# A projection's 64-row rests, run as pairs on both halves of the array

## The chip, the cores and the metric

The kernel runs on one core of one Trainium2 chip. The metric is device time in microseconds (us) of one execution. Of the kernel before, three timed runs gave a median of 467.6 us (466.76 to 468.47).

Engines by the profile's names: PE is TensorE's matmul, PEld its weight load, DVE is VectorE, ACT is ScalarE, POOL is GpSimd, SP is SyncE, which issues nearly all the DMAs. PE works with 128 rows of the array, or with the rows split into halves (64) or quarters (32); a matmul on a part of the rows leaves the other parts free for another.

## The reference

Two blocks in sequence over x of 2048 tokens and width 576, both on a layer-normed input with a residual:

```python
h  = x + attention(layernorm(x))      # 32 heads of width 18
h2 = h + mlp(layernorm(h))            # 576 -> 4608, gelu, -> 576
# attention, per segment s of 512 tokens (4 in all):
#   logits = q k^T * 18**-0.5 + causal mask ; a_dot = softmax(logits) v
#   a_mem  = phi(q) M / (phi(q) z + 1e-6)     phi(t) = t + 1 if t > 0 else exp(t)
#   o = sigmoid(beta) * a_mem + (1 - sigmoid(beta)) * a_dot
#   then M += phi(k)^T v,  z += sum phi(k)
#   attention = concat(o) @ wo,  with q, k, v = x @ wq, x @ wk, x @ wv
```

All arrays are bfloat16. The width of 576 matters here: it is four blocks of 128 and a rest of 64, and every product over the width (q, k, v, wo, the MLP's first layer) has such a rest.

## The kernel before

**Tiling.** The tokens are cut into 8 chunks of 256 (two tiles of 128). Two chunks make one segment of the attention. A chunk passes through these streams, each a Python generator that issues operations:

- `stream_P(tl)`: layer norm of a token tile (DVE, with POOL for the power), its transpose `xT` (for the first two chunks through PE and a copy, from the third on by a transposing DMA, `dma_t`), and the q, k, v projection. The output is 1728 columns wide. The first chunk cuts it into 6 pieces of 288 columns, all later ones into 4 pieces of 432 (`CH`). A piece is five matmuls into one PSUM bank: `mm5` (line 549) issues four with 128 rows (line 551) and one for the rest (line 552). This last one has 65 rows (`KTAIL`) and not 64: row 64 of the weights is a row of zeros, and with 65 rows the matmul counts as one over the whole array. The piece is then copied out of the bank by ACT or DVE (`move`, lines 631 and 632), into `qk_pad` and `v_aug`; q and k are transposed into `QT` and `KT`.
- `stream_A`: the attention. `scores` (line 752) computes 16 small matmuls on 32 rows each, four side by side; ACT takes the exponential of all of them (line 758, 2048 columns); POOL or DVE masks; `weighted` (line 784) multiplies with v. `memory_mm` (line 807) and `stream_M` (line 710) are the memory's reads and updates.
- `stream_B(tl)`: the product with wo (also `mm5`), residual, second layer norm and its transpose.
- `stream_F1`, `stream_F2`: the MLP's two layers. F1 takes its rests first, in pairs on 64 rows: `tails` (line 1048) lets the upper and the lower half of the rows work at the same time, each into its own bank; then come four matmuls of 128 rows for each (line 1061). For this the upper rows, 64 to 127, hold a second copy of the rest of the input: the second layer norm (line 573) writes its last 64 columns twice. F1 of the first chunk is done by lines 1021 and 1023, F2 by line 1110.

**PSUM.** There are 8 banks: four for the scores (`st`), one for the attention's sums (`ox`) and three (`bank0` to `bank2`) that all other products share. After the last attention the four score banks join those three as `late`.

**The order.** A planner (`step`, lines 1135 to 1183) runs all streams against estimated durations and due times (`SLACK`, `PHASES`) and picks each engine's next operation. It also chooses the bank of each product (`bank_slots.take()`). Where PE would have nothing to do early on, it puts in fillers (line 1179), matmuls of 256 columns over a zeroed tile `pq`. Then `arranged` (line 1197) moves operations by a table (`MOVES`): pairs of numbers, the operation and the one after which it goes; an operation can also go to another engine this way. What results is one fixed order for each engine, and each engine works through its own in that order.

Of the kernel before, what the change touches and what calls it, by code (L numbers as in the profile page):

```python
# [9 lines left out]
ALU = mybir.AluOpType  # L10
# [6 lines left out]
def kernel(  # L17
# [41 lines left out]
    def sbuf(name, shape, dt=BF16):  # L59
# [77 lines left out]
    MOVES = dict(PE=[74, -1, 71, 73, 77, 71, 81, 78, 75, 81, 85, 75, 89, 80, 93, 89, 86, 82, 90, 84, 83, 88, 97, 83, 94, 97, 102,  # L137
# [30 lines left out]
                                      ACT=[59, 53, 61, 54, 45, 113, 124, 120, 135, 124, 55, 130, 155, 145, 168, 171, 224, 218, 56,  # L168
# [7 lines left out]
                                      DVE=[18, 14, 24, 40, 17, 24, 30, 31, 36, 32, 101, 36, 35, 33, 19, 35, 39, 41, 46, 39, 139,  # L176
# [71 lines left out]
    port_op = [None]  # L248
    fetched = []
    writer, readers, known = {}, {}, {}  # L250

    class Op:
        start, end, at, apart, two, hold, ways = None, NEVER, None, False, False, 0.0, None

# [1003 lines left out]
```

## Time and profile before

| | before |
|---|---|
| median of three runs | 467.6 us (466.76 to 468.47) |
| profiled execution | 467.02 us |
| its span, first to last instruction | 465.1 us |
| PE busy | 459.2 us (99%), 6102 matmuls |
| ACT busy | 320.0 us (69%) |
| DVE busy | 272.9 us (59%) |
| POOL busy | 180.0 us (39%) |
| mean share of the DMA engines, GB/s | q1: 69.7%; 174 GB/s |

A group line of the profile names the line of the kernel, the engine, the operation, what it writes and reads, the shapes, the count (x), and then the busy time, the mean duration of one in ns and the idle time ahead of it. PE's matmuls are pipelined: one lasts longer than the distance to the next, so that the busy time of a group is no sum of durations, and the distance of two starts in the timeline tells what a matmul costs the stream. Each timeline line merges neighbours of one kind and has start, time covered, engine, line, operation, what is written and read, shapes and count.

### The profile page before, as it was taken

What the parts mean: (1) busy time and instruction counts of PE and PEld (TensorE: products, weight loads), DVE (VectorE), ACT (ScalarE), POOL (GpSimd) and SP (SyncE); (2) the same over time, 40 slices, a digit from 0 to 9 for tenths busy, and PEclk for the clock granted to TensorE, in tenths of its full rate; (3) what the DMA queues carried; (4) which work ended last, traced back from release to release, by engine and by line L of the source; (5) the groups of instructions that cost most, each with busy time, mean ns of one, the idle gap of its engine ahead of it and who ended that gap; (6) DMA issues with size and microseconds to landing.
All of it is one profiled execution on the core that took longest, in us unless ns stands there. A gap on an engine that the chain in (4) does not pass through costs nothing.

```text
span 465.1 us, 14420 instructions
## 1 busy us (share of the span) xinstructions
PE 459.2 (99%) x6102; PEld 351.6 (76%) x6102; DVE 272.9 (59%) x712; ACT 320.0 (69%) x299; POOL 180.0 (39%) x240
## 2 busy tenths in 40 slices
PE   8999999999999999999999999999999999999997
PEld 6777787777677777767677777678778788888885
DVE  4889878787874355777755647687345524212020
ACT  3987788977888877966768778658778453423620
POOL 4567233778563144487442116474233401000000
PEclk9999999999999999999999999999999999999999
DMA  8889699887598557587876645989956595747211
GB/s 210 251 257 293 127 205 192 177 216 153 130 220 205 167 148 222 129 164 150 152 178 184 176 154 149 169 192 196 229 168 178 167 215 169 155 126 222 68 40 51
DMA packets 123152, 80.89 MB, mean 174 GB/s; under 512 B 57536, under 2 KB 121040, under 8 KB 123088
## 3 DMA queue, kind: packets, MB, share of 16 engines
q1 hardware_dynamic: 123056, 79.98, 69.7%
q8 instruction: 47, 0.77, 0.7%
q0 software_dynamic: 32, 0.01, 0.1%
q14 instruction: 17, 0.14, 0.1%
HBM read 60.03 MB, written 7.08 MB: 144 GB/s over the span
## 4 chain that ended last, share of the span: by engine, by line
PE 96%; DMA 2%; DVE 1%; SPq 0%; issue 0%
PE bank L1110 25%; PE bank L1061 22%; PE bank L551 14%; PE ox L784 7%; PE st L752 6%; PE late L1110 5%; PE late L1061 4%; PE bank L1048 4%; PE bank L552 3%; DMA wqkv<-in_A_wq_dram 2%; PE bank L1021 1%; PE ox L1110 1%; PE bank L807 1%; PE bank L670 1%; PE ox L1061 1%; PE bank L710 1%
## 5 line engine op out<-in xcount | busy, mean ns | idle before, releaser
L758 ACT ACTIVATE pt<-st 128x2048 bf16<-128x2048 f32 x80 | 150.2, 1878 | 56.8 <-PE st L752 51.5
L1110 PE MATMUL bank<-w_sb,hT 128*128 128x288 bf16 x936 | 135.9, 286 | 0.0
L1110 PEld LDWEIGHTS <-hT 128*128 128x128 bf16 x1152 | 109.1, 98 | 26.9 <-issue 1.1
L1071 DVE TENSOR_TENSOR hT<-bank,b1T 128x512 bf16<-128x512 f32 x78 | 53.8, 689 | 69.0 <-PE bank L1061 68.5
L1061 PE MATMUL bank<-xn2T,w1g 128*128 128x256 bf16 x688 | 87.9, 273 | 0.0
L1061 PEld LDWEIGHTS <-w1g 128*128 128x128 bf16 x768 | 70.6, 98 | 16.0 <-issue 6.7
L763 POOL TENSOR_SCALAR_AFFINE_SELECT pt<-pt 128x512 bf16<-128x512 bf16 x84 | 54.1, 657 | 71.2 <-ACT pt L758 66.3
L1083 ACT ACTIVATE hT<-hT 128x1536 bf16<-128x1536 bf16 (+3 forms) x24 | 66.0, 2764 | 16.4 <-DVE hT L1071 16.2
L551 PE MATMUL bank<-wqkv,xT 128*128 128x432 bf16 (+1 forms) x268 | 57.1, 336 | 0.7 <-DMA wqkv<-in_A_wq_dram 0.7
L551 PEld LDWEIGHTS <-xT 128*128 128x128 bf16 x400 | 36.5, 97 | 19.7 <-issue 0.9
L784 PEld LDWEIGHTS <-pt 128*128 128x128 bf16 x1280 | 42.2, 96 | 4.5 <-issue 0.6
L784 PE MATMUL ox<-v_aug,pt 128*128 128x19 bf16 x1280 | 44.1, 172 | 0.0
L752 PE MATMUL st<-QT,KT 32*128 32x128 bf16 x1280 | 32.4, 217 | 0.6 <-issue 0.6
L799 POOL TENSOR_TENSOR pq<-ek,pq 128x512 bf16<-128x512 bf16 x24 | 27.9, 1162 | 12.6 <-DVE ek L797 10.8
L752 PEld LDWEIGHTS <-KT 32*128 32x128 bf16 x1280 | 18.5, 92 | 16.2 <-issue 14.3
L829 POOL TENSOR_TENSOR o_nat<-t,t 128x288 bf16<-128x288 f32 x24 | 19.9, 830 | 25.7 <-DVE t L828 25.6
L1069 ACT ACTIVATE hT<-bank,b1T 128x256 bf16<-128x256 f32 x62 | 25.8, 473 | 5.6 <-PE bank L1061 4.6
L1061 PEld LDWEIGHTS <-wqkv 128*128 128x128 bf16 x272 | 26.0, 98 | 4.5 <-issue 0.4
L1110 PE MATMUL late<-w_sb,hT 128*128 128x288 bf16 x180 | 25.0, 286 | 0.0
L795 POOL TENSOR_SCALAR pq<-QT 128x512 bf16<-128x512 bf16 x24 | 15.4, 641 | 24.7 <-PE bank L807 9.9
L569 POOL TENSOR_TENSOR rstd_b<-rstd_b,mhalf 128x1 f32<-128x1 f32 x16 | 9.6, 602 | 39.2 <-DVE rstd_b L564 39.2
L931 POOL TENSOR_TENSOR h_t<-h_t,b_bc 128x576 f32<-128x576 f32 x16 | 20.7, 1296 | 6.0 <-DVE xn L573 4.8
(136 smaller groups left out, 620.1 us busy)
## 6 DMA issues: line engine op xcount, KB each, us to landing
w1g<-in_B_w_dram SPq DMA_DIRECT2D x50, 512.0 KB, 4.3
wqkv<-in_B_w_dram SPq DMA_DIRECT2D x17, 512.0 KB, 4.1
w_sb<-in_B_w_dram SPq DMA_DIRECT2D x6, 864.0 KB, 6.0
hd<-h_t SPq DMA_DIRECT2D x16, 288.0 KB, 3.0
hc<-hd SPq DMA_DIRECT2D x32, 144.0 KB, 2.8
w1g<-in_B_w_dram SPq DMA_DIRECT2D x100, 32.0 KB, 3.1
x_b<-in_A_x_dram SPq DMA_DIRECT2D x18, 144.0 KB, 3.7
hT<-in_B_w_dram SPq DMA_DIRECT2D x5, 512.0 KB, 5.6
```

What stands on the lines that cost most here:

```text
L551: nc.tensor.matmul(out=out_ap, lhsT=lhsT_of(slice(0, P), k), rhs=rhs_of(slice(0, P), k), start=(k == 0), stop=False)
L752: nc.tensor.matmul(out=st4[:, i, n * P:(n + 1) * P], lhsT=KTs[(c - c % 2 + kt // 2) % 3][rows, g, (kt % 2) * P:(kt % 2 + 1) * P], rhs=QTs[ ...
L758: op("ACT", 1.88, lambda: nc.scalar.activation(out=pt[:], in_=st4[:], func=ACT.Exp, scale=scale), sk, [("pt", slot, n) for n in range(4)], ...
L763: either(("POOL", 0.64, lambda part=part: nc.gpsimd.affine_select(out=part, in_=part, pattern=[[0, 4], [1, P]], compare_op=ALU.is_ge, fill ...
L784: nc.tensor.matmul(out=oxv[:, 4 * (g % 4) + i, :], lhsT=pts[slot][:, i, n * P:(n + 1) * P], rhs=v_augs[(2 * s0 + kt) % 6][:, 4 * g + i, :] ...
L799: op("POOL", 1.16, lambda: nc.gpsimd.tensor_tensor(out=pq[:], in0=e_g, in1=pq[:], op=ALU.add), ["ek"], ["pq"], slack=SLACK["add"])
L931: op("POOL", 1.29, lambda: nc.gpsimd.tensor_tensor(out=h_t[:], in0=h_t[:], in1=b2_bc[:], op=ALU.add), ["b2"], [("h", tl)], slack=SLACK["hb"])
L1061: nc.tensor.matmul(out=banks[b][:, a * Q:(a + 1) * Q], lhsT=w1_main(wt)[:, k, (2 * (h % 2) + a) * P:(2 * (h % 2) + a + 1) * P], rhs=xn2T[c ...
L1069: nc.scalar.activation(out=hT[:, f + a, :], in_=banks[b][:, a * Q:(a + 1) * Q], func=ACT.Identity, bias=b1T[:, f + a:f + a + 1])
L1071: either(("DVE", 0.69, lambda hT=hT, f=f, b=b: nc.vector.tensor_tensor(out=hT[:, f:f + 2, :], in0=banks[b][:].rearrange("p (a w) -> p a w" ...
L1083: op("ACT", (f1 - f0) * Q * 0.00083 + 0.18, lambda hT=hT, f0=f0, f1=f1: nc.scalar.activation(out=hT[:, f0:f1, :], in_=hT[:, f0:f1, :], fun ...
L1110: nc.tensor.matmul(out=acc, lhsT=hT[:, q, tl * P:(tl + 1) * P], rhs=w2_sb[:, q, hs], start=(q == 0), stop=(q == NF - 1))
```

## The change

It has four parts.

1. **Pairs.** From the third chunk on (`NP = 2`), the rests of two neighbouring pieces of the projection run together: one on rows 0 to 63, the other on rows 64 to 127, each into its own bank, ahead of the four matmuls of 128 rows of either piece. So the second piece's bank is taken before the first piece's main products. For this the layer norm of the projection writes its last 64 columns twice, as the second layer norm did before (`again`), and three loads bring the rests of the weights' second and fourth piece into rows 64 to 127 of `wqkv`, in place of the zero row. They are issued once the second chunk's products, which still read that row, are done.
2. **Banks by a table.** The planner still takes banks, but which of the three a product gets is decided afterwards by a string of digits (`PLACE`), one for each use; `bank(k)` looks it up when the instruction is issued.
3. **Fillers.** A list (`DROP`) takes 32 of the 53 fillers out.
4. **Order.** The table `MOVES` is new for all five engines; some copies, bias additions and masks also change between ACT, DVE and POOL by it. PE has 6070 matmuls in place of 6102.

```diff
-    MOVES = dict(PE=[74, -1, 71, 73, 77, 71, 81, 78, 75, 81, 85, 75, 89, 80, 93, 89, 86, 82, 90, 84, 83, 88, 97, 83, 94, 97, 102,
...
+    MOVES = dict(PE=[104, 74, 85, 104, 73, 86, 80, 73, 97, 80, 91, 97, 201, 91, 184, 201, 100, 184, 96, 100, 98, 94, 187, 98,
...
+    DROP = [71, 72, 73, 74, 75, 76, 77, 79, 81, 84, 86, 88, 89, 93, 98, 102, 105, 106, 107, 108, 116, 117, 158, 182, 183, 185,
+            186, 187, 201, 203, 204, 206]
+    PLACE = ("2020212002211112102211010001200212102101102122001201021202212201022102102012012120210202102201021021"
...
+    uses, place = [], {}
+
+    def bank(k):
+        return banks["bank", place[k.serial]] if isinstance(k, Bank) else banks[k]
...
-    LATER, AHEAD, NS, MOST = 0, 5, 1, 3
+    LATER, AHEAD, NS, MOST, NP = 0, 5, 1, 3, 2
...
-            for to, f0, f1 in ((0, 0, D), (D, 512, D))[0:2 if f32 else 1]:
+            for to, f0, f1 in ((0, 0, D), (D, 512, D))[0:2 if again else 1]:
...
-                layernorm(who, xt[:], xk, xn1[tl], xnk, False, SLACK["lnp"])
+                layernorm(who, xt[:], xk, xn1[tl], xnk, False, SLACK["lnp"], c >= NP)
...
+                def main(lo=lo, hi=hi, b=b, xTt=xTt):
+                    for k in range(4):
+                        nc.tensor.matmul(out=bank(b)[:, 0:CH], lhsT=xTt[:, k, :], rhs=wqkv[:, k, lo:hi], start=False, stop=(k == 3),
+                                         skip_group_check=True)
+
+                if c < NP:
+                    op("PE", 5 * mm(hi - lo), product, [kx] + wk, [b], n=10)
+                else:
+                    if ch % 2 == 0:
+                        pair = []
+
+                        def rests(pair=pair, lo=lo, xTt=xTt):
+                            for h in range(2):
+                                rows = slice(64 * h, 64 * h + 64)
+                                nc.tensor.matmul(out=bank(pair[h])[:, 0:CH], lhsT=xTt[rows, 4, :], rhs=wqkv[rows, 4, lo + h * CH:lo + (h + 1) * CH],
+                                                 start=True, stop=False, skip_group_check=True)
...
+                    op("PE", 5 * mm(CH), main, [kx] + wk, [b], n=10).true = 4 * mm(CH)
...
+                    if c == NP - 1 and (c, 1 - tl) in half_V:
+                        for j, W in enumerate((A_wq, A_wk, A_wv)):
+                            for n0, n1 in ((CH, 2 * CH), (3 * CH, 4 * CH)):
+                                a0, a1 = max(n0, j * D), min(n1, (j + 1) * D)
+                                if a0 < a1:
+                                    o = dma(0, lambda W=W, j=j, a0=a0, a1=a1: nc.sync.dma_start(
+                                        out=wqkv[64:P, 4, a0:a1], in_=W[512:576, a0 - j * D:a1 - j * D]), (), [("wqkv_up", a0)]).by
...
-        return order
+        return [o for o in order if o.made not in DROP]
```

In the changed kernel the pairs stand at line 702, the main products at 690, the earlier pieces at 594 and 595, the scores at 843, `weighted` at 875, F1's rests at 1141, F1's main products at 1154, F2 at 1203 and the fillers at 1272.

More of the change, by code (lines that the diff above doesn't have):

```diff
@@ L250, with own, also, mark @@
     writer, readers, known = {}, {}, {}
+    class Bank(tuple):
+        serial = None
+    def own(k):
+        return ("use", k.serial) if isinstance(k, Bank) else k
+    last, users = {}, {}
+    def also(o, rd, wr):
+        rd, wr = [own(k) for k in rd], [own(k) for k in wr]
+        o.inner += [last[k] for k in rd if k in last]
+        for k in wr:
+            o.inner += [*([last[k]] if k in last else []), *users.get(k, ())]
+        mark(o, rd, wr)
+    def mark(o, rd, wr):
+        for k in map(own, wr):
+            last[k] = o
+            users[k] = []
+        for k in map(own, rd):
+            users.setdefault(k, []).append(o)
     class Op:
-        start, end, at, apart, two, hold, ways = None, NEVER, None, False, False, 0.0, None
+        start, end, at, apart, two, hold, ways, opens, true, rows = None, NEVER, None, False, False, 0.0, None, (), None, None
         def __init__(self, eng, dur, issue, preds, due, table=None, after=None):
             self.eng, self.dur, self.issue, self.preds, self.due, self.table = eng, dur, issue, preds, due, table
-            self.made = len(ops)
+            self.made, self.inner, self.uses = len(ops), [], []
             self.after = after
@@ L298, in op @@
         o.n, o.mode = n, mode
+        also(o, rd, wr)
+        o.uses = [k.serial for k in (*rd, *wr) if isinstance(k, Bank)]
         o.port = eng == "POOL" if port is None else port
@@ L615, in stream_P @@
                 b = bank_slots.take()
-                bank = banks[b]
-                op("PE", 0.28, n=10, issue=lambda bank=bank: transposes5(xn1[tl], bank), rd=[xnk, (*xnk, "pad"), "ident"], wr=[b])
-                either(("ACT", 0.69, lambda bank=bank, xTt=xTt: nc.scalar.copy(out=xTt[:], in_=tview(bank))),
-                       ("DVE", 0.47, lambda bank=bank, xTt=xTt: nc.vector.tensor_copy(out=xTt[:], in_=tview(bank))), [b], [kx])
+                op("PE", 0.28, n=10, issue=lambda b=b: transposes5(xn1[tl], b), rd=[xnk, (*xnk, "pad"), "ident"], wr=[b])
+                either(("ACT", 0.69, lambda b=b, xTt=xTt: nc.scalar.copy(out=xTt[:], in_=tview(b))),
+                       ("DVE", 0.47, lambda b=b, xTt=xTt: nc.vector.tensor_copy(out=xTt[:], in_=tview(b))), [b], [kx])
                 bank_slots.give(b)
@@ L628, in stream_P @@
             parts = {0: [(*qkk, "pad")], 1: [(*qkk, "pad")]}
+            wk_all = [f"wqkv{j}" + e for j in range(3) for e in ("", "t")] + ["wqkv_pad"]
             def move(dst, src, n, key):
-                either(("ACT", n * 0.00083 + 0.16, lambda: nc.scalar.copy(out=dst, in_=src)),
-                       ("DVE", n * 0.00104 + 0.16, lambda: nc.vector.tensor_copy(out=dst, in_=src)), [b], [key])
+                either(("ACT", n * 0.00083 + 0.16, lambda: nc.scalar.copy(out=dst, in_=src())),
+                       ("DVE", n * 0.00104 + 0.16, lambda: nc.vector.tensor_copy(out=dst, in_=src())), [b], [key])
             for ch, (lo, hi) in enumerate(cuts):
@@ new lines, in main @@
+                def main(lo=lo, hi=hi, b=b, xTt=xTt):
[12 more added lines that the diff above has]
+                                                 start=True, stop=False, skip_group_check=True)
+                        rest = op("PE", 0.0, rests, [kx] + wk_all, [], n=0)
+                        rest.true, rest.rows = mm(CH), 64
+                        rest.inner += wqkv_up
+                    pair.append(b)
+                    if isinstance(b, Bank):
+                        rest.uses.append(b.serial)
+                        mark(rest, [], [b])
+                    else:
+                        also(rest, [], [b])
+                    op("PE", 5 * mm(CH), main, [kx] + wk, [b], n=10).true = 4 * mm(CH)
@@ L893, in stream_B @@
                 b = bank_slots.take()
-                bank = banks[b]
-                op("PE", 0.28, n=10, issue=lambda bank=bank, c=c: transposes5(o_nats[c % 2][:, tl, :], bank), rd=ok + ["ident"], wr=[b])
-                either(("ACT", 0.69, lambda bank=bank, xTt=xTt: nc.scalar.copy(out=xTt[:], in_=tview(bank))),
-                       ("DVE", 0.47, lambda bank=bank, xTt=xTt: nc.vector.tensor_copy(out=xTt[:], in_=tview(bank))), [b], [kx])
+                op("PE", 0.28, n=10, issue=lambda b=b, c=c: transposes5(o_nats[c % 2][:, tl, :], b), rd=ok + ["ident"], wr=[b])
+                either(("ACT", 0.69, lambda b=b, xTt=xTt: nc.scalar.copy(out=xTt[:], in_=tview(b))),
+                       ("DVE", 0.47, lambda b=b, xTt=xTt: nc.vector.tensor_copy(out=xTt[:], in_=tview(b))), [b], [kx])
                 bank_slots.give(b)
@@ L916, in stream_B @@
                 b = bank_slots.take()
[L917 to L920 removed]
+                op("PE", 0.28, n=10, issue=lambda b=b: transposes5(xn2[tl], b), rd=[("xn2", tl), "ident"], wr=[b])
+                either(("ACT", 0.69, lambda b=b, xn2T_part=xn2T_part: nc.scalar.copy(out=xn2T_part, in_=tview(b))),
+                       ("DVE", 0.47, lambda b=b, xn2T_part=xn2T_part: nc.vector.tensor_copy(out=xn2T_part, in_=tview(b))),
                    [b], [("xn2T", c % 4, tl)])
@@ L1047, in tails @@
                                 rows = slice(64 * h, 64 * h + 64)
-                                nc.tensor.matmul(out=banks[bs[2 * i + h]][:, a * Q:(a + 1) * Q],
+                                nc.tensor.matmul(out=bank(bs[2 * i + h])[:, a * Q:(a + 1) * Q],
                                                  lhsT=w1s[i][0][rows, 4 * 512 + a * P:4 * 512 + (a + 1) * P], rhs=xn2T[c % 4][rows, 4, :],
@@ L1178, in step @@
             b = bank_slots.take()
-            op("PE", 0.213 if now < 4 else 0.11, lambda: nc.tensor.matmul(out=banks[b][:, 0:Q], lhsT=pq[:, 0, :], rhs=pq[:, 2:4, :],
+            op("PE", 0.213 if now < 4 else 0.11, lambda: nc.tensor.matmul(out=bank(b)[:, 0:Q], lhsT=pq[:, 0, :], rhs=pq[:, 2:4, :],
                                                                         start=True, stop=True), ["pq"], [b])
@@ L1209, in arranged, with wait @@
                 line[e].insert(line[e].index(ops[after]) + 1 if after >= 0 else 0, o)
+        place.update(enumerate(map(int, PLACE)))
+        left, held, begun = [0] * len(uses), {}, set()
+        for o in ops:
+            for u in o.uses:
+                left[u] += 1
+        def wait(o):
+            if not all(p in at for p in o.inner) or any(left[held[place[u]]] for u in o.uses if u not in begun and place[u] in held):
+                return NEVER
+            return max([0.0] + [at[p] + (0.0 if p.eng == o.eng else LAT[p.eng]) for p in o.inner])
         order, at, free = [], {}, dict.fromkeys(line, 0.0)
         while any(line.values()):
-            can = []
-            for e, l in line.items():
-                if l and all(p in at for p in l[0].preds):
-                    can.append((max([free[e]] + [at[p] + (0.0 if p.eng == e else LAT[p.eng]) for p in l[0].preds]), l[0].made, e))
-            t, i, e = min(can)
+            t, i, e = min((max(free[e], wait(l[0])), l[0].made, e) for e, l in line.items() if l)
+            assert t < NEVER
             o = line[e].pop(0)
-            at[o] = free[e] = t + o.end - o.start
+            at[o] = free[e] = t + (0.0 if o.made in DROP else o.end - o.start if o.true is None else o.true)
             if hasattr(o, "moves"):
                 at[o.moves] = t + o.moves.end - o.start
+            for u in o.uses:
+                begun.add(u)
+                held[place[u]] = u
+                left[u] -= 1
             order.append(o)
-        return order
+        return [o for o in order if o.made not in DROP]
     EN = mybir.EngineType
```

114 lines of the change are left out of this document (64 added, 50 removed), and 200 rows, old and new, of tables (ACT, DVE, MOVES, POOL).

## The prediction

> **What bounds the kernel now.** I read the page first, then what TensorE (PE) waits for, then its groups by shape, then its timeline. The page gives the span and the share of each engine; the chain of work that ended last lies almost wholly on PE:
>
> ```profile
> span 465.1 us, 14420 instructions
> ...
> PE 459.2 (99%) x6102; PEld 351.6 (76%) x6102; DVE 272.9 (59%) x712; ACT 320.0 (69%) x299; POOL 180.0 (39%) x240
> ...
> PE 96%; DMA 2%; DVE 1%; SPq 0%; issue 0%
> ```
>
> This is all that PE waited for in the whole span, by the view of waits (engine, line, releaser: us, times, longest):
>
> ```profile
> PE ox L1179 <- DVE pq L508: 1.3, 1, 1.3
> PE bank L551 <- DMA wqkv<-in_A_wq_dram: 0.7, 1, 0.7
> PE st L752 <- issue: 0.6, 1, 0.6
> ```
>
> So an edit is worth what it takes from PE's own stream of issues. Busy time hides that stream, since matmuls overlap; it has to be read from start to start. The groups by shape give a projection matmul's full duration, and the timeline (start, us, work) the distances:
>
> ```profile
> L551 PE MATMUL bank<-wqkv,xT 128*128 128x432 bf16 x224 | 50.1, 346 | 0.0
> ...
> L552 PE MATMUL bank<-wqkv,xT 65*128 65x432 bf16 x56 | 19.5, 348 | 0.0
> ```
> ```profile
> 71.36 0.22 PE L1023 MATMUL bank<-xz,hT 128*128 128x128 bf16 x1
> 71.51 0.39 PE L1048 MATMUL bank<-xn2T,w1g 64*128 64x256 bf16 x4
> 71.84 1.05 PE L1061 MATMUL bank<-xn2T,w1g 128*128 128x256 bf16 x8
> 72.82 0.40 PE L752 MATMUL st<-QT,KT 32*128 32x128 bf16 x16
> 73.15 1.05 PE L1061 MATMUL bank<-xn2T,w1g 128*128 128x256 bf16 x8
> ```
> ```profile
> 6.56 0.50 PE L1179 MATMUL ox<-pq 128*128 128x256 bf16 x2
> ...
> 7.94 0.38 PE L1179 MATMUL bank<-pq 128*128 128x256 bf16 x2
> 8.99 0.65 PE L551 MATMUL bank<-wqkv,xT 128*128 128x288 bf16 x4 [0.67 <-DMA wqkv<-in_A_wq_dram]
> ...
> 20.20 0.60 PE L1179 MATMUL bank<-pq 128*128 128x256 bf16 x4
> ...
> 21.67 0.82 PE L1179 MATMUL bank<-pq 128*128 128x256 bf16 x6
> 22.32 0.35 PE L784 MATMUL ox<-v_aug,pt 128*128 128x19 bf16 x8
> ```
>
> Five prices follow. A 432-column matmul issues every 0.183 us: four run from 25.09 to 25.82 in the timeline, and the last one to the next group takes 0.18 to 0.19. It costs that on 128 rows and on 65 alike (346 and 348 ns long). Going from 128 rows to 64 or 32 adds about 0.092: L1023 to L1048 is 0.15 where its pitch is 0.058. Leaving 64 or 32 rows adds about 0.11: L1048's four 256-column matmuls, two at a time, take 0.33 where two passes of 0.109 take 0.22; L752's sixteen take 0.33 where four passes of 0.0558 take 0.22. Passing from 32 rows straight to 64 costs that 0.11 once. A filler (L1179) costs 0.109 from 6.56 on and 0.213 before. With these prices, I summed PE's whole order from the first projection product at 8.99 to the last issue at 461.97: 451.0 of the 453.0 us. The other 2.0 are waits: 0.85 and 0.30 between 43 and 49, the rest in steps of under 0.1. From 49.24 to 366.39 the sum drifts by 0.55 only, so PE does not wait in the body.
>
> **The change, part by part.** Counts are from the instruction orders of both kernels.
>
> Pairs: from the third chunk on, 6 chunks x 2 tiles x 2 pairs = 24 pairs; 48 rests take the place of 48 passes, two per pass. Out: 24 x 0.183 = -4.39.
>
> Row changes: PE's order had 230 changes of row tiling, and has 271. 17 more leave 128 rows (x 0.092 = 1.56), 24 more leave 32 or 64 rows (x 0.11 = 2.64): +4.20. A lone rest pays two changes (0.20), more than it saves. 15 of the 24 adjoin a group of scores, and pay one; but 8 first-layer rests (L1048) that adjoined scores no longer do. So the edit that names the change is worth -0.2. The nearest row is L1048, itself a pair of 64-row matmuls, so I take its price. The bounds are 0.075 per entry (L784 before L752: 0.49 against 0.41) and 0.10 (eight of L1061: 0.98 against 0.88), which leave -0.5 to 0.0.
>
> The Trainium skill, TensorEngine Tiling (Array Packing), section Key Properties, says that a change of tiling mode drains TensorE. The trace agrees that a change costs, but at 0.09 to 0.11, less than the 0.165 by which a matmul's 348 ns outlasts its pitch; by a full drain of that length at each of 41 more changes the sum would be +2.4 in place of -0.2.
>
> Fillers: the table DROP leaves out 32 of 53. Before the first product (8.99, set by the load of wq that was issued at 1.73) they cost nothing either way, while the clock lasts (below). After it 17 become 4: 13 x 0.109 = -1.42. This is a gain only if real work stands ready there. It partly does: before the third score group the new order has 10.46 us of real PE work in place of 11.13, before the fifth 16.1 for 16.6, before the seventh 23.06 for 22.56, the fourth and sixth the same.
>
> Waits: between two score groups lies one exponential (L758, 1.88 us). The least distance, end to start, that PE passed without a wait is 2.29. The new order has 1.67 (second to third) and 1.88 (at 40 us of PE work) in it: +0.62 and +0.41. Against that stand the 1.15 us between 43 and 49, where the chain runs over DVE's two layernorms; this place is rearranged too. Bounds: both stay (+1.0) or all 2.0 us of waits go (-2.0). I take their exchange, 0, since 1.03 and 1.15 are the same size.
>
> Work that lies beside PE, costed at nothing: DVE gets 12 copies of 64 columns (L573 run twice). Nearest rows: 0.085 (a 128x32 memset) and 0.475 (the 64-column L573 of 32-bit input), so 1 to 5.7 us over 240 us, on an engine that is 59% busy. What covers them is the time between a transfer's landing and its use, some 2 us at 48 us (L323 issued at 45.13, 3.0 to land, used at 50.43); where that is gone, each costs up to its 0.475 on PE.
>
> SP gets three loads of wqkv's lower rows, 18 to 55 KB. Each waits until PE has done the second chunk's products, which read the zero row; behind them on SP's queue stand w1, w2, and transposes for the third chunk. The last of those reads comes near 35 us, the first pair near 50, and the longest load of wqkv so far took 8.6. If the cover went, the first pair would wait. The bank table (PLACE) issues nothing.
>
> Sum: -0.19 - 1.42 + 0 = **-1.6**. The profiled execution took 467.02 (465.1 and 1.9 around the span), 0.6 under the median of 467.6. On its own footing the forecast is 465.4; against the median **466.0**.
>
> **Rivals.** (1) *The clock starts late*, ending on the other side. The fillers from 1.25 on issue every 0.213 us, and every 0.109 from 6.56 on: the full rate came after 5.3 us of unbroken work, though the granted clock in the windows reads 1.00 throughout. The new order has 8 fillers (1.7 us, from about 1.9, as five memsets go ahead of pq's on DVE), then nothing until xn is there (its write ends at 5.50), then 5 transposes and 10 fillers to about 8.1, then the gap to 8.99. If only unbroken work counts, it starts anew at 8.99 and ends at 14.3, and PE loses half of 5.3: 466.0 + 2.65 = 468.7. It decides from 3.2 us at half rate on, which take the whole 1.6. For: three gaps where there was none. Against: PE is still at work in over half of the time from 5.5 on.
>
> The Trainium skill, TensorE: Matmul & The Clock Gate, Part 1, states that the clock doubles after a busy window of about 3.4 us that runs freely. The trace agrees that the rate doubles under work, with 5.3 us; by that rule an estimate of the loss is up to 3.4 (half of two windows, by where an edge falls after 8.99), against my 0.
>
> (2) *Banks are short*: a pair must have two of three banks free at once, and holds the second for four main products (0.73) before it is written on. Against: the least PE work between a bank's last write and its next is 0.82 in the new order, 0.87 in the old, and 1.01 before a pair; an eviction needs about 0.85 (the product's last issue ends at 23.54, ACT's cast of it 23.75 to 24.27, 0.1 to PE). For: ACT and DVE must be free at that moment. At 0.1 to 0.3 us per pair, 24 pairs give +2.4 to +7.2: 468.4 to 473.2, likeliest 469.6.
>
> (3) *The pairs do not run side by side*: +24 x 0.183 = 470.4. Against: the pairs of L1048 start 0.01 apart.
>
> (4) *The new order waits less*: all 2.0 us of waits go, 464.0.
>
> **How the numbers follow.** About 0.3% (1.4 us) is what a measurement of this kernel can tell from no change: faster means under 466.2, slower over 469.0. The forecast has 0.53, with 465.0 to 467.0 as its own range (waits 1 us either way); about three quarters of that chance counts as faster (0.40), since the two tight gaps are already in it, the rest as same (0.13). The late clock has 0.17: same 0.13, slower 0.04 with some wait on top. Banks 0.17: slower 0.14, same 0.03. Side by side 0.05, slower. Fewer waits 0.08, faster. Together faster 0.48, same 0.29, slower 0.23. The range from 464.2 to 469.6 leaves out the upper half of banks, the serial pairs and the very best of the waits.
>
> **What would show it.** Pairs: the 432-column rests on 64 rows start 0.01 apart, the next main product 0.29 later (0.183 and 0.11). Row changes: scores followed by a rest still take 0.33. Fillers: from 8.99 on, PE has no idle time but some 0.6 before the third scores. Clock: the first products' pitch is 0.12 us, not 0.24. Banks: no wait of PE on DVE or ACT at the rests. The prediction is wrong if PE's waits grow by more than 1 us, or if the first products run at half rate.

## The result, and the profile after

Slower. The changed kernel took 471.1 us (median of seven runs, 469.35 to 471.69), the kernel before on the same chip 467.7. The ratio is 1.0067, with a 95% interval of 1.0050 to 1.0084, so 2.3 to 3.9 us are lost. The forecast was 466.0, within 464.2 to 469.6: the sign is wrong, and the miss is 5.1 us.

The profiled execution took 471.29 us. The page of the changed kernel, with span, busy time and the chain that ended last:

```profile
span 469.6 us, 14391 instructions
...
PE 457.0 (97%) x6070; PEld 345.2 (74%) x6070; DVE 265.3 (56%) x710; ACT 325.3 (69%) x317; POOL 178.5 (38%) x242
...
PE 83%; DMA 8%; DVE 3%; POOL 2%; SPq 2%; issue 1%; ACT 1%; POOLq 0%
```

PE is busy for 2.2 us less than before, as it has less to do, but its share of the chain fell from 96% to 83%. Transfers and DVE now stand in between. This is what PE waited for (engine, line, releaser: us, times, longest):

```profile
PE bank L1272 <- DVE pq L551: 1.9, 1, 1.9
PE bank L627 <- DVE xn L616: 1.8, 1, 1.8
PE bank L594 <- DMA xT<-o_nat: 1.5, 2, 1.1
PE bank L1141 <- DVE stats_p L602: 0.8, 1, 0.8
PE bank L702 <- DMA xT<-xn: 0.8, 1, 0.8
PE bank L1141 <- DMA w1g<-in_B_w_dram: 0.7, 2, 0.5
PE ox L875 <- POOL pt L854: 0.5, 1, 0.5
PE bank L1154 <- DMA w1g<-in_B_w_dram: 0.4, 1, 0.4
PE bank L1114 <- ACT KT L763: 0.2, 1, 0.2
```

The first line stands ahead of all work, as before. The second is the gap before the first transposes, which the forecast had seen in the order. The others are new: before, PE waited in its body for 0.6 us only. The fourth line (0.8) is a transfer too: the timeline shows PE's weight load there waiting 0.97 us for first-layer weights, which landed 0.05 before these matmuls started. They do not read `stats_p`; its work on DVE only ended at about that time.

The pairs themselves look as forecast, in the timeline (start, us, work) and in the groups by shape:

```profile
61.23 0.40 PE L843 MATMUL st<-QT,KT 32*128 32x128 bf16 x16
61.56 0.36 PE L702 MATMUL bank<-wqkv,xT 64*128 64x432 bf16 x2
61.85 0.90 PE L690 MATMUL bank<-wqkv,xT 128*128 128x432 bf16 x4
62.59 0.39 PE L1114 MATMUL bank<-xn2T,w1g 128*128 128x128 bf16 x4
```
```profile
L690 PE MATMUL bank<-wqkv,xT 128*128 128x432 bf16 x192 | 40.8, 347 | 0.0
...
L702 PE MATMUL bank<-wqkv,xT 64*128 64x432 bf16 x48 | 8.6, 353 | 0.8 <-DMA xT<-xn 0.8
```

The scores take 0.33 up to the next start. The two rests together cover 0.36 where one lasts 353 ns, so they start 0.01 apart, and the main products follow 0.29 later. The last column says that all the idle time ahead of the rests was for a transfer: PE never waited there for DVE or ACT, that is for a bank.

The timeline of the head shows what did not go as forecast:

```profile
2.75 1.06 PE L1272 MATMUL bank<-pq 128*128 128x256 bf16 x4
5.60 0.71 PE L627 MATMUL bank<-ident,xn 128*128 128x128 bf16 x5 [1.79 <-DVE xn L616]
...
8.02 1.17 PE L594 MATMUL bank<-wqkv,xT 128*128 128x288 bf16 x4
8.98 0.45 PE L595 MATMUL bank<-wqkv,xT 65*128 65x288 bf16 x1
9.22 0.73 PE L594 MATMUL bank<-wqkv,xT 128*128 128x288 bf16 x4
```

The first product takes 1.20 from start to start (8.02 to 9.22), where before it took 0.61. The transposes at 5.60 and the fillers behind them run at half rate too. So the full rate comes 3.8 us after the start of the transposes and not with the first product.

In sums: PE starts its first product 0.97 earlier than before (wq's load landed earlier) and by the forecast has 1.6 less work to issue. Against this stand 0.65 at half rate, 0.5 more after the end of PE's last matmul (3.6 for 3.2), and, as what is left of the 4.5 between the two spans, 5.9 more of waits behind the first product. The view of waits lists 4.3 of these (4.9 against 0.6). It counts a wait from the end of a matmul, which outlasts its pitch, so it shows less.

### The profile page after: what moved, and what is told of

The parts are those of the page before. It is cut to its first block, busy times and chain, and to the rows that moved or that the text cites. A ratio compares the mean times of both kernels' runs of the same rounds, so it can differ in the third digit from the quotient of the medians.

```text
span 469.6 us, 14391 instructions
## 1 busy us (share of the span) xinstructions
PE 457.0 (97%) x6070; PEld 345.2 (74%) x6070; DVE 265.3 (56%) x710; ACT 325.3 (69%) x317; POOL 178.5 (38%) x242
## 3 DMA queue, kind: packets, MB, share of 16 engines
q1 hardware_dynamic: 123296, 80.09, 71.4%
## 4 chain that ended last, share of the span: by engine, by line
PE 83%; DMA 8%; DVE 3%; POOL 2%; SPq 2%; issue 1%; ACT 1%; POOLq 0%
PE bank L1203 22%; PE bank L1154 19%; PE bank L690 7%; PE ox L875 5%; PE bank L594 5%; PE late L1203 5%; DMA w1g<-in_B_w_dram 4%; PE st L843 4%; PE late L1154 4%; PE bank L1141 3%; PE bank L702 1%; DMA xT<-xn 1%; DMA wqkv<-in_B_w_dram 1%; PE bank L595 1%; PE bank L1114 1%
## 5 line engine op out<-in xcount | busy, mean ns | idle before, releaser
L1164 DVE TENSOR_TENSOR hT<-bank,b1T 128x512 bf16<-128x512 f32 x73 | 50.1, 689 | 69.4 <-PE bank L1154 69.1
L1176 ACT ACTIVATE hT<-hT 128x1536 bf16<-128x1536 bf16 (+3 forms) x24 | 65.5, 2765 | 0.1
L1162 ACT ACTIVATE hT<-bank,b1T 128x256 bf16<-128x256 f32 x72 | 30.1, 472 | 26.7 <-PE bank L1154 25.8
L690 PE MATMUL bank<-wqkv,xT 128*128 128x432 bf16 x192 | 40.8, 347 | 0.0
L690 PEld LDWEIGHTS <-xT 128*128 128x128 bf16 x192 | 16.1, 97 | 15.2 <-issue 4.5
L1207 DVE TENSOR_TENSOR ot<-bank,hc 128x288 bf16<-128x288 f32 x26 | 11.8, 456 | 25.2 <-PE bank L1203 20.2
L594 PEld LDWEIGHTS <-xT 128*128 128x128 bf16 x208 | 19.2, 99 | 8.9 <-DMA xT<-o_nat 2.1
```

Source lines behind the costliest of these rows:

```text
L594: nc.tensor.matmul(out=out_ap, lhsT=lhsT_of(slice(0, P), k), rhs=rhs_of(slice(0, P), k), start=(k == 0), stop=False)
L690: nc.tensor.matmul(out=bank(b)[:, 0:CH], lhsT=xTt[:, k, :], rhs=wqkv[:, k, lo:hi], start=False, stop=(k == 3), skip_group_check=True)
L1162: nc.scalar.activation(out=hT[:, f + a, :], in_=bank(b)[:, a * Q:(a + 1) * Q], func=ACT.Identity, bias=b1T[:, f + a:f + a + 1])
L1164: either(("DVE", 0.69, lambda hT=hT, f=f, b=b: nc.vector.tensor_tensor(out=hT[:, f:f + 2, :], in0=bank(b)[:].rearrange("p (a w) -> p a w", ...
L1176: op("ACT", (f1 - f0) * Q * 0.00083 + 0.18, lambda hT=hT, f0=f0, f1=f1: nc.scalar.activation(out=hT[:, f0:f1, :], in_=hT[:, f0:f1, :], fun ...
```

## The experiments

Times are medians of the runs of each kernel, and the ratios are against runs of the kernel before on the same chip, which had 467.3 to 467.8. A second reading is used throughout: the start of each of the 80 groups of scores on PE, compared between the profiled executions of two kernels with the same order. A difference that stays is carried along, and a jump is a wait that only one of the two had.

### Undoing the pairs

```diff
-                            for h in range(2):
+                            for h in range(0):
...
-                    op("PE", 5 * mm(CH), main, [kx] + wk, [b], n=10).true = 4 * mm(CH)
+                    op("PE", 5 * mm(CH), product, [kx] + wk, [b], n=10).true = 4 * mm(CH)
...
-                                    o = dma(0, lambda W=W, j=j, a0=a0, a1=a1: nc.sync.dma_start(
-                                        out=wqkv[64:P, 4, a0:a1], in_=W[512:576, a0 - j * D:a1 - j * D]), (), [("wqkv_up", a0)]).by
+                                    o = dma(0, lambda: None, (), [("wqkv_up", a0)]).by
```

> The order of after, with the pairs undone: each piece of the projection is five matmuls over 128 and 65 rows again, as before; the three loads into rows 64 to 127 are not issued. Theory T (the pairs do what was forecast, and the loss comes from the new order, in which transfers and copies land later than PE needs them): PE's work grows, since 24 passes come back (24 x 0.183 = +4.39) and row changes go (9 pairs with two each at 0.20, 15 beside scores with one at 0.11: -3.45), by +0.9, and PE's waits stay near 8.4 us; 471 to 473.5, likeliest 472.0. Theory P (the pairs, or the second bank that they hold, cause the waits): PE's waits fall back to about 2 us, and the time to 467 or less.

It took 471.3, ratio 1.0077 (1.0053 to 1.0100). The loss stays, so the pairs are not its cause, and theory P falls. The scores start 1.10 later than in the changed kernel from the first group on (its half rate lasted longer, to 11.6) and 1.89 later from the 64th: +0.8 between them, waits that only one of the two had included. The medians, 471.3 and 471.1, do not show it. DVE's 12 copies stay in this kernel.

### Removing fillers alone

```diff
+            fillers.append(len(ops))
...
-        return order
+        seen = [o.made for o in order if o.made in fillers]
+        return [o for o in order if o.made not in seen[36:]]
```

> The kernel before, without the 17 fillers that stand after the first projection product; nothing else is changed. The forecast's step on fillers holds: 17 x 0.109 = -1.85, 465.8. Rival: real work does not stand ready where they stood, and PE waits for as long: 467.6, with 1.5 us or more of new waits of PE between 9 and 50 us in the profile.

469.4, ratio 1.0035 (1.0015 to 1.0055): slower than before, which neither side expected. In its profiled execution (467.94) the scores start 1.74 earlier than before at the third group, so the 1.85 is won at first. It is then given back in small waits, 0.4 at 120 us, 0.4 at 154, 0.6 at 327, until PE is 0.3 behind: for transposes, for xn2T, for DVE's output. PE got ahead, and what it needs did not. This execution is the fastest of the ten, 1.5 under their median, so it shows where the gain goes, and not the whole loss.

### Filling the gap

```diff
-            o.issue()
+            for _ in range(10 if o.made == 184 else 1):
+                o.issue()
```

> After, with one early filler issued ten times, so that PE works through its gap from 3.7 to 5.6 us ahead of the first transposes. If the gap set the clock back (the late clock): the first product after them runs at a 0.12 pitch, takes 0.6 in place of 1.2, and the time falls by 0.6, to 470.5. If the gap has nothing to do with it: the first product stays at 1.2 us, and the time at 471.1 or up to 0.2 above.

468.0, ratio 1.0013 (0.9988 to 1.0037): five times what was expected. Nine idle matmuls bring the changed kernel back to the time of before. Its timeline:

```profile
2.74 2.60 PE L1272 MATMUL bank<-pq 128*128 128x256 bf16 x13
5.60 0.45 PE L627 MATMUL bank<-ident,xn 128*128 128x128 bf16 x5 [0.26 <-DVE xn L616]
...
7.40 0.65 PE L594 MATMUL bank<-wqkv,xT 128*128 128x288 bf16 x4 [0.37 <-DMA wqkv<-in_A_wq_dram]
```

The transposes already run at the full rate (0.45, not 0.71), and the first product starts at 7.40 and takes 0.61. At the first scores PE is 1.28 ahead of the changed kernel, at the 22nd 2.78, at the last 4.01. So in this execution (466.82, 1.2 under the median) about a third of the gain is at the head, and the rest is waits in the body that do not come up.

### A late load behind a transpose

```diff
+        sp = line["SP"]
+        i = max(j for j in range(len(sp) - 1) if sp[j].moves.dur == 864 and sp[j + 1].dur == 1.25)
+        sp[i:i + 2] = sp[i + 1], sp[i]
```

> After, with one change on SP's queue: the last 864 KB load of w2, which is issued at 49.8, and the transpose of the third chunk's second tile behind it (issued 51.7, landed 57.7) change places. Theory T: the transpose lands some 2 us sooner, PE's wait of 0.78 us at 57.7 goes, and the time falls by 0.5 to 0.9, to 470.4, if no later wait takes it up. Theory P or a plain lack of transfer rate: the landing stays at 5 us or more, or the same 0.8 is waited for elsewhere, 471.1.

469.6, ratio 1.0051 (1.0033 to 1.0069), which overlaps that of the changed kernel: unclear. The wait at 57.7 is gone, but PE waits 0.55 at 60.3 for the next transpose, of o_nat, which now stands closer behind the load. With the gap filled as well, the same swap gave this:

> After with the gap filled and the last 864 KB load behind the transpose that stood next to it. Gap alone gave 467.98, the load alone 469.58 against 471.12. If both effects are real and separate, 466.5, less than before; if the load's 1.5 was chance, 468.

467.4, ratio 0.9996 (0.9980 to 1.0013): not told apart from 468.0, and not the 466.5. The load's effect is not shown to be real; its profile has a wait of 1.2 at 59 for that transpose.

### The gap alone, in the kernel before

```diff
-        return order
+        seen = [o.made for o in order if o.made in fillers]
+        return [o for o in order if o.made not in seen[13:29]]
```

> The kernel before, with 16 of its fillers taken out between 4.2 us and the first transposes, so that PE has there the gap that the order of after has; nothing else is changed. Theory C (a gap in PE's early work sets its full rate back, as 3.6 to 5.9 us after the gap in the three profiles with it so far): the first products run at half rate until 9.5 to 12, and the kernel loses 0.5 to 1.6 us: 468.0 to 469.2. Rival (the gap does nothing, the gain of nine fillers in it came from elsewhere): the first product keeps its pitch of 0.12, 467.5.

472.0, ratio 1.0093 (1.0075 to 1.0111): the gap alone, here 1.35 us long, costs 4.6, more than the whole change. The timeline shows half rate up to about 12 us:

```profile
5.56 0.71 PE L582 MATMUL bank<-ident,xn 128*128 128x128 bf16 x5 [1.35 <-DVE xn L573]
...
8.52 1.12 PE L551 MATMUL bank<-wqkv,xT 128*128 128x288 bf16 x4 [0.75 <-DMA wqkv<-in_A_wq_dram]
...
9.67 1.16 PE L551 MATMUL bank<-wqkv,xT 128*128 128x288 bf16 x4
```

Theory C had the mechanism and the place, with too small a price. At the first scores PE is 1.1 behind the kernel before, as expected. 3.0 more come in the body. The view of PE's waits has seven lines there, 3.6 in all, where the kernel before has one of 0.6. The two longest are a transpose and DVE:

```profile
PE bank L551 <- DMA xT<-o_nat: 1.2, 2, 0.8
...
PE bank L551 <- DVE ox L820: 0.7, 1, 0.7
```

### Light transfers

From the sixth on, each 512 KB load of the first layer's weights brings only its first quarter; these kernels leave out the other three quarters of those weights.

```diff
-        dma(512, lambda: nc.sync.dma_start(out=w1_main(wt), in_=B_w1[0:512, fcols].rearrange("(k p) f -> p k f", p=P)), (), [k], SLACK["w1"])
+        kk = 4 if n < 5 else 1
+        dma(512, lambda: nc.sync.dma_start(out=w1_main(wt)[:, 0:kk, :], in_=B_w1[0:P * kk, fcols].rearrange("(k p) f -> p k f", p=P)), (), [k], SLACK["w1"])
```

> After, in which from the sixth on each load of 512 KB of the MLP's first layer brings only its first quarter (the other three quarters of these weights are left out, PE multiplies with what stands there). All instructions stay, and the transfers move about 28% less. Theory T (transfers that queue behind each other make PE wait in the body): the medians from issue to landing of the transposes fall to 3 us or less, PE's waits after 50 us fall from 5.8 to under 2, and the time by 3 to 4, to 467 to 468. Rival (the waits come from the order on DVE, POOL and ACT, or from the clock): 470 or more.

> The same loads cut to their first quarter in the kernel before (the other three quarters of these weights are left out), as the measure for the run on after. PE waits for transfers only once there (0.7 at the head), so theory T and its rival both expect 466.5 to 467.5. The difference of after and before, both with light loads, is by theory T -1 to +0.5 (work -1.6, the late clock +0.6 to +1.9), and by the rival +2.5 or more.

After 469.1 (ratio 1.0038, 1.0024 to 1.0053), before 466.3 (0.9974, 0.9963 to 0.9985). Bytes moved fall from 80.1 to 53.7 MB, and the transposes' landings shorten (QT from 5.0 to 3.7), but both kernels gain: 2.0 and 1.1. The difference stays at 2.8, so theory T, that the transfers' weight makes the difference, fails for most of it; the time lies between what theory T and its rival expected. What the light loads took from the changed kernel are its waits at 57.7 and after 86 us. One wait stayed and grew, 1.89 at 83.5 for the transpose of o_nat; so that one is no matter of bytes.

Light loads were then put under the other two edits of the kernel before, and under the filled gap:

> The kernel before, both without the 17 fillers after the first product and with the light loads (three quarters of those weights are left out). Theory T2 (removing fillers brings PE forward by 1.7, and transfers that are not forward catch it later): against before with light loads the 1.85 of the step on fillers is kept, 465 to 465.7. Rival (what catches it is another engine, or the gap in the early work): 467 or more.

466.5, against 466.3 with light loads alone: the 1.85 is not kept here either. This time most of it goes at the head, and the last 0.4 at 121. The first product starts at 8.71 (8.57 with light loads alone), and PE waits 0.34 for wk's load, 0.66 at 21 to 22 for DVE and POOL, 0.55 at 44. Fillers stood where real work was not ready.

> The kernel before with the same gap in PE's early work (16 fillers out), and with the light loads (three quarters of the MLP's first-layer weights from the sixth load on are left out). Against before with light loads (466.3). Theory A (the late clock costs 1.1 at the head, and the rest of the 4.6 that the gap cost with full loads are waits for transfers, in which PE, moved against them, catches on heavy queues): with light loads 1.0 to 1.8 are left, 467.3 to 468.1. Rival (the loss has nothing to do with the transfers): 4 or more, 470.3 and above.

468.9, ratio 1.0030 (1.0004 to 1.0056), the runs from 466.0 to 472.1: 2.6 above light loads alone, where the gap cost 4.6 with full loads. That lies between the two expectations, nearer to A. Against the profiled execution with light loads alone, this one is 2.3 behind at the first scores (half rate to 13, the first product 0.5 later) and loses 0.6 more in the body, where with full loads it was 1.1 and 3.0. So, as far as one profile of each shows, most of the later loss hangs on the weights' transfers, and the loss at the head does not.

> After with the gap filled (one early filler ten times) and with the light loads (the same three quarters left out): both suspects away. If clock and transfers are all that the forecast missed, its sum holds against before with light loads (466.3 - 1.6): 464.7, within 1. If the new order has waits of its own besides (POOL's mask at 19, DVE's copies at 80, up to 2.5 together): 466.5 or more.

467.1, ratio 0.9987 (0.9972 to 1.0002): 2.4 above the forecast on this footing. With the clock and the transfers out of the way, the new order has waits of its own: 1.3 for the transpose of o_nat, 0.5 for one of xn, 0.5 for a mask on POOL, 0.2 for ACT and 0.2 for QT.

### The order on SP's queue

First all transposes, each moved ahead of the weight load directly before it, with the gap filled:

```diff
+        sp = line["SP"]
+        for o in [o for o in sp if o.dur == 1.25]:
+            i = sp.index(o)
+            for _ in range(1):
+                if i and sp[i - 1].dur == 0.5 and sp[i - 1].moves.dur in (45, 512, 864):
+                    sp[i - 1:i + 1] = [o, sp[i - 1]]
+                    i -= 1
```

> After with the gap filled, and on SP's queue every transpose moved ahead of the one w1 or w2 load that stands directly before it. Theory T (transposes wait on the weights' transfers): their medians from issue to landing fall from 3.1 to 4.2 us to 3.5 or less, and the time by up to 1.5, to 466.5. Rival (loads come later in turn, and PE waits for them): 468 or more, with PE waiting for w1g.

474.7, ratio 1.0159 (1.0123 to 1.0196), the slowest of all. PE waits 2.5 for a w1 load at 190 us, as the rival said, and 2.5 for a transpose of o_nat at 59. The wait at 59 has a price beside its length. The timeline and the windows (stretch, its length, PE busy, granted clock, DMA share, GB/s):

```profile
61.59 0.67 PE L594 MATMUL bank<-wo_t,xT 128*128 128x288 bf16 x4 [2.52 <-DMA xT<-o_nat]
62.09 0.40 PE L595 MATMUL bank<-wo_t,xT 65*128 65x288 bf16 x1
62.29 1.16 PE L594 MATMUL bank<-wo_t,xT 128*128 128x288 bf16 x4
...
192.66 1.48 PE L1154 MATMUL bank<-xn2T,w1g 128*128 128x256 bf16 x12 [2.46 <-DMA w1g<-in_B_w_dram]
193.98 0.35 PE L875 MATMUL ox<-v_aug,pt 128*128 128x19 bf16 x8
```
```profile
61.50:62.00 0.50, 0.41 (x4) 1.00 1.29 311
62.00:62.50 0.50, 0.50 (x5) 0.62 1.09 356
62.50:63.00 0.50, 0.50 (x3) 0.50 1.10 348
...
65.00:65.50 0.50, 0.50 (x3) 0.50 0.24 46
65.50:66.00 0.50, 0.50 (x7) 0.96 0.00 0
```

PE starts at the full rate, drops to half 0.5 us later, and stays there for 3.4 us (62.1 to 65.5): 1.7 more are lost. The wait at 190, as long, has no such price: the twelve matmuls behind it start 0.11 apart (192.66 to 193.98), which is the full rate.

Then one transpose only, that of o_nat which PE waited for at 81 to 84. These are the lines of SP's queue (start, us for the issue) in the changed kernel:

```profile
78.13 1.24 SPq L357 DMA_TRANSPOSE xT<-xn  x1
79.41 0.58 SPq L516 DMA_DIRECT2D x_p<-in_A_x_dram  x1
80.09 1.97 SPq L357 DMA_TRANSPOSE xT<-o_nat  x1
```

and this is the chain that ended last at that place (start, us, what):

```profile
79.25 0.69 DVE hT L1164
79.94 0.15 DVE stats_p L602
80.09 3.58 DMA xT<-o_nat
83.68 0.05 issue
83.72 0.66 PE bank L594 x4
```

DVE had written o_nat by 78.2. Its transpose was issued 1.9 later, behind a load of x and a transpose that PE needs only at 86.9, and PE waited for it to land. The chain's step over DVE's `stats_p` is no cause: on SP's queue the load of x was issued until 79.99, and the transpose followed at 80.09.

```diff
+        sp = line["SP"]
+        t = [o for o in sp if o.dur == 1.25]
+        sp.remove(t[8])
+        sp.insert(sp.index(t[7]), t[8])
```

> The same with only the second of the two changes on SP's queue (o_nat's transpose at 81 to 84). Theory O: the first products with wo after 80 us wait no longer for it, -0.7: 467.3. Rival: DVE's copies, which PE waited for at 80, hold PE as long, 468.0.

466.0, ratio 0.9959 (0.9943 to 0.9975): faster than before by 1.2 to 2.7 us, and 2.0 better than with the gap alone filled, where 0.7 was expected. In the two profiles the difference is 1.5, and 1.0 of it is the wait itself, a jump of the scores at the 22nd group. SP's queue and all that PE still waits for:

```profile
76.95 1.38 SPq L357 DMA_TRANSPOSE xT<-o_nat  x1
78.37 1.27 SPq L357 DMA_TRANSPOSE xT<-xn  x1
```
```profile
PE bank L1272 <- DVE pq L551: 1.9, 1, 1.9
PE ox L875 <- POOL pt L854: 0.5, 1, 0.5
PE bank L1114 <- ACT KT L763: 0.2, 1, 0.2
PE bank L702 <- DMA xT<-xn: 0.2, 1, 0.2
```

With the 864 KB load moved behind two transposes besides:

```diff
+        w2 = max((o for o in sp if o.moves.dur == 864), key=sp.index)
+        sp.remove(w2)
+        sp.insert(sp.index(t[2]) + 1, w2)
```

> After with the gap filled, and two changes on SP's queue: the last 864 KB load goes behind the next two transposes, and the transpose that PE waited for at 81 to 84 us (of o_nat, issued behind a transpose and an x load that nobody waits for yet) goes ahead of these two. Theory O (the rest of the miss is waits that the new order has of itself, because single transposes are issued late): the wait at 81 to 84 (0.7 to 1.9 in the runs so far) and that at 56 to 59 go, and against the 468.0 with the gap alone filled 1 to 1.5 are won: 466.5 to 467.0; the forecast of 466.0 is missed only by the masks at 19. Rival (such waits move on, as with every transpose moved): 468 or more.

466.4, ratio 0.9971 (0.9950 to 0.9992): nothing beside the one transpose, within the intervals. In light loads:

> The first of these two with light loads (three quarters of the MLP's first-layer weights left out from the sixth load on), against before with light loads (466.3) and after with the gap filled and light loads (467.1). If clock, transfers and the order's own waits are together all that the forecast missed, its sum of -1.6 is nearly reached: 464.7 to 465.5. If something is still missing, 466.3 or more.

464.5, ratio 0.9924 (0.9900 to 0.9949). On the light footing the forecast's sum gives 466.3 - 1.6 = 464.7. With gap and transposes mended, it is reached, but not by its terms: against light loads alone, 1.7 of the 2.4 between the two profiles is an earlier first product (6.87 for 8.57).

### The fourth corner, and the pairs once more

> After with only the one transpose moved on SP's queue, the gap in PE's early work left as it is: the fourth corner of the square (neither 471.1, gap filled 468.0, both 466.0). If the two losses are separate, 2.0 is won and 469.1 is left, the gap costing 3.1 still. If the late clock costs only because it moves PE against that transpose, 466.5 to 467.5: then the clock's own price is the 0.6 to 1.9 at the head.

468.7, ratio 1.0027 (1.0013 to 1.0042). The square in medians:

| | transpose late | transpose moved |
|---|---|---|
| gap open | 471.1 | 468.7 |
| gap filled | 468.0 | 466.0 |

The gap costs 3.1 or 2.7, the transpose 2.4 or 2.0. By the ratios and their intervals each of these is good to 1.0 to 1.4 us only, so that the two losses look separate within that, no closer. Their sum is 5.1, as large as the whole miss. In this corner's profile half rate ended early, at 8.6, and PE was 0.6 behind the mended kernel at the first scores. The rest of the gap's 3.3 between these two spans came later: 1.1 for a transpose at 57, 0.7 for DVE at 371 and 0.65 for a transpose at 380.

> After with the gap filled and the transpose moved (466.0), and with the pairs undone as in the first experiment. Theory: pairs as forecast; undoing them costs 24 x 0.183 less 3.45 of row changes, +0.9: 466.9, with PE's scores after 306 us later by 0.9 to 1.0. Rival (the pairs cost through their second bank): 466.0 or less.

466.35, ratio 0.9975 (0.9963 to 0.9986), against 0.9959 (0.9943 to 0.9975) with pairs: the times alone don't tell them apart. The scores do: PE is 0.20 behind at the first group (half rate to 7.8) and 1.10 at the 80th. These 0.9, some 0.2 of them a wait at 56.7, answer to the expected 0.94.

## Why the prediction was wrong

**Row changes and pairs: right.** The rests run side by side, a pair costs 0.29 up to the next main product, no bank is waited for, and undoing the pairs costs 0.7 to 0.9 of PE's time for an expected 0.94. The other price that the prediction worked out, a full drain of 0.165 at each change, would have made undoing them a gain of 1.1 (4.39 against 33 changes): the runs stand against that here. The other 8 of the 41 changes, at first-layer rests, were not undone in any run.

**Fillers: the step failed in its place ahead of the first product.** The forecast said that fillers there "cost nothing either way, while the clock lasts (below)", and took the clock for a rival with 0.17. It was the main case. The gap that their removal left costs 2.7 to 3.1 in the changed kernel and 4.6 in the kernel before. The rival named the mechanism, but neither the place nor the price. It let the clock start anew at a gap before 8.99; what counted was the stop from 3.8 to 5.6. And it counted half rate alone (up to 2.65), of which the changed order's profiles with the gap show 0.3 to 1.8 behind the first product. The larger part is waits in the body that come after it. What was said of the fillers behind the first product, -1.42 "only if real work stands ready there", was too high for the order of before, where taking them out lost time. What they are worth in the new order no run tells by itself.

**Waits: the exchange of 0 failed, by one transpose.** The forecast looked for the new waits between the scores and at the rearranged layer norms. Of its two tight gaps the first came true (0.63 ahead of the third scores, 0.47 of it the mask on POOL), the second with 0.3 ahead of the 12th. What cost 2.0 to 2.4 in medians was at 80 us, where o_nat's transpose stands behind two transfers of SP's queue. Its wait is 1.1 in the changed kernel's profile; where the rest of the price arises was not found.

**Work beside PE: SP was looked at for the wrong change.** "SP gets three loads" was the whole step on SP; these were covered as said. But the new order table also moves every transpose and load on SP's queue, and none of these moves was priced. DVE's 12 copies took 0.49 each, where 0.085 to 0.475 was the bound, and no wait is put down to them; no run takes them out.

**Sum: reached once the two are mended, and partly by luck.** With gap and transpose away the kernel takes 466.0 (forecast 466.0), and its profiled execution 465.35 (forecast 465.4). But the forecast had the first product at 8.99 in both kernels and took 1.6 out of what follows. In these two profiles the first product starts 1.25 earlier (7.74 for 8.99), and from there to the end of PE's last matmul only 0.4 is saved (452.6 for 453.0). If the 1.6 of work is gone, about 1.2 of waits came in its place, where the forecast had 0, and an earlier start that it did not have made up for them.

What stays open is why a late head costs so much later. That most of it goes with light loads shows that the transfers have a part in it. Removing fillers, which brings PE forward, brought small waits too. So the kernel before loses by being moved in either direction, but what in its timing avoids these waits was not found.

## What to carry to other kernels

Fillers ahead of the first real work are not idle work: before one is removed, see whether PE would stand still before it has reached its full rate. Stops of 1.4 and 1.8 us cost 3 to 5 us here, and nine matmuls of 0.2 us won about 3 back. Where an order is rewritten, go through the queue that issues the transfers, one by one, for a transfer that stands behind others that nobody waits for yet. Moving the one such transpose won 2 us here, and moving every transpose by one place lost 7. A saving on a busy PE counts only where what it needs next comes earlier as well.

## What the runs showed of the hardware

- **Half rate after a short gap.** With 1.8 us idle before 5.6, PE took another 3.0 to 6.0 us to reach the full rate in the five profiles of the new order with the gap, each time another. In the two of the order before with a gap of 1.35 it took 6.4 and 7.5. The twelve profiles without such a gap took 2.9 to 5.9 from PE's first matmul, so the gap makes PE start over. In the middle of the kernel, a wait of 2.5 us was enough for 3.4 us at half. The Trainium skill, TensorE: Matmul & The Clock Gate, Part 1, states that the clock gate works in free-running windows of about 3.4 us, and that an idle one closes it. The trace agrees with the length of 3.4, but the wait that closed it was shorter, 2.5. Length alone does not decide: in the same run 2.46 us at 190 did not lower the rate. The clock records in that run's trace change at 62.12 and 65.54 us, one step of 3.41 apart, and in all 19 traces a stretch at full rate lasts a whole number of such steps. An estimate by counting on from 65.54 puts the wait at 59 wholly inside one step (58.7 to 62.1) and an edge, at 191.8, into the wait at 190. One case of each does not prove that this is what decided.
- **The granted clock does not always show it.** The windows read 0.50 in the middle of the kernel, but 1.00 over the first 10 us, where matmuls issued at half rate. This 1.00 is no measurement: the changed kernel's trace has no record of the clock before 9.36 us, where the full rate begins, and the view shows 1.00 where it has none. There only the pitch tells. The prediction read this 1.00 as the granted clock.
- **Transfers and time.** A third less traffic (80.0 to 53.6 MB) took 1.1 us (0.7 to 1.7) off the kernel before, whose PE waited for transfers for 0.7 us only.
